# A channel gate streamed in one pass: an 8-row first tile, 26 equal tiles and a TensorE loop

## The chip, the cores and the metric

The kernel runs on one core of a Trainium2 chip. A time is the device time of one execution in microseconds (us), and where several runs are given, it is their median. A profiled execution shows, for every engine and every DMA queue, when each piece of work began and ended. Its span runs from the first to the last instruction of the program and is a little shorter than the time.

## The reference

The input `x` is a bf16 image of 384 x 384 pixels with 384 channels, 113 MB. The output multiplies each channel by a gate that depends on the channel's mean over all pixels:

```python
    g = jnp.einsum("bhwc->bc", x) / (H * W)
    ...
    for i in range(k):
        s = s + gp[:, i:i + C] * w1d[i]
    s = _sigmoid(s)
    return x * s[:, None, None, :]
```

Here `k` is 1, so the gate is `sigmoid(mean * w1d[0])`. All of `x` must be read for the mean before the right gate is known, and all of `x` must be multiplied by it. [...]

## The kernel before

**Layout.** The 147,456 pixels are spread over 128 partitions, which makes 1,152 "rows": one row is one pixel (384 channels, 768 bytes) in each partition. A tile of n rows is a block of n x 128 pixels, and each partition holds n x 768 contiguous bytes of it. The tiles lie in one big buffer, `arena`, in six slots of 44 rows each. Before the change there are 27 tiles: 25 of 44 rows, then one of 28 and one of 24 (`sizes`, line 165).

**An early gate and a check.** The kernel reads and writes the image once. From the first tile alone it forms an early gate, `s_early`, and multiplies every tile with it as it passes. Meanwhile it sums all the other tiles too. At the end it forms the true gate, `s_true`, and compares the two bit for bit, after rounding to bf16. If they differ anywhere, a flag (`redo`) makes SyncE, VectorE and ScalarE run a second pass that loads the whole image again, multiplies it with the true gate and stores it over the first result. The instructions of this second pass (planner `again`, lines 341 to 352) stand behind an `If` in each of the three programs.

**The work of a tile.**
- Load: a DMA from the image to the slot. The first four tiles (`BOTH`, line 115) are loaded in two halves, one issued by SyncE and one by ScalarE; the others are loaded whole by SyncE (`load`, line 169).
- Sum: TensorE multiplies the tile by a matrix of ones in pieces of 512 columns, which adds over the partitions and accumulates in three PSUM banks (`add_rows`, line 199; the matmuls are recorded at line 187). A tile of 44 rows is 33 matmuls. Tile 0 has banks of its own (group 0); all other tiles accumulate in group 1.
- Gate and store: VectorE multiplies the tile by `s_early` (`gate`, line 156, recorded at line 159), in its own slot, and ScalarE issues the DMA that stores it (`put`, line 234). The very last tile is gated into another slot.
- After the sums of a group, VectorE adds the three banks into 384 columns (`add_banks`, line 219), and ScalarE takes the sigmoid (lines 288 and 312). The lines 320 to 334 form the flag.

**What sets the order.** The `Planner` (line 14) holds a list of instructions for each engine. It records for every row of the arena who wrote it last and who has read it since, and puts a wait ahead of an instruction for each of those it depends on (`_needs`, `_wait`). The lists are then written out unrolled: each engine's program is one straight run, with no loop. [...] The loop of line 297 records, for tile k, the gate and store of tile k-6, the load of tile k into the slot that this store sets free, and the sum of tile k. SyncE's queue thus carries loads, and ScalarE's queue carries the halves of the first four tiles, the small weight `w_one`, and then the stores.

Of the kernel before, what the change touches and what calls it, by code (L numbers as in the profile page):

```python
# [13 lines left out]
class Planner:  # L14
# [9 lines left out]
    def __init__(self, nc, name, n_dma_sems):  # L24
        self.nc = nc
        self.streams = {e: [] for e in ("sync", "scalar", "vector", "tensor", "gpsimd")}
        self.sems = {e: nc.alloc_semaphore(f"{name}_{e}") for e in self.COMPUTE}
        self.count = {e: 0 for e in self.COMPUTE}
        self.pool = [nc.alloc_semaphore(f"{name}_dma_{i}") for i in range(n_dma_sems)]
        self.pool_uses = [0] * n_dma_sems  # L30
        self.n_dma = 0
        self.writer = {}
        self.readers = {}
        self.seen = {e: {} for e in self.streams}
        self.final = []

    def _wait(self, engine, token):
        sem, value = token
        if self.seen[engine].get(sem.name, 0) >= value:
            return  # L40
        self.seen[engine][sem.name] = value
        self.streams[engine].append(("wait", sem, value))

    def _needs(self, reads, writes):
        need = {}
        tokens = []
        for r in reads:
            if r in self.writer:
                tokens.append(self.writer[r])
        for r in writes:  # L50
            if r in self.writer:
                tokens.append(self.writer[r])
            tokens.extend(self.readers.get(r, ()))
        for sem, value in tokens:
            if need.get(sem.name, (None, 0))[1] < value:
                need[sem.name] = (sem, value)
        return list(need.values())

    def _record(self, token, reads, writes):
        for r in reads:  # L60
# [5 lines left out]
    def op(self, engine, emit, reads=(), writes=(), signal=True):  # L66


        reads, writes = list(reads), list(writes)
        for token in self._needs(reads, writes):  # L70
            if engine == "tensor" and token[0].name == self.sems["tensor"].name:
                continue
            self._wait(engine, token)
        token = (self.sems[engine], self.count[engine] + 1)
        if signal:
            self.count[engine] += 1
        self.streams[engine].append(("op", emit, self.sems[engine] if signal else None, 1))
        self._record(token, reads, writes)

    def dma(self, engine, out, in_, reads=(), writes=()):  # L80
        reads, writes = list(reads), list(writes)
        for token in self._needs(reads, writes):
            self._wait(engine, token)
        i = self.n_dma % len(self.pool)
        self.n_dma += 1
        if self.pool_uses[i]:
            self._wait(engine, (self.pool[i], 16 * self.pool_uses[i]))
        self.pool_uses[i] += 1
        token = (self.pool[i], 16 * self.pool_uses[i])
        self.streams[engine].append(  # L90
            ("op", lambda e: e.dma_start(out, in_), self.pool[i], 16)  # L91
        )
        self._record(token, reads, writes)
        return token

    def emit(self, name, e, most=None):

        now = self.streams[name][:most]
        del self.streams[name][: len(now)]
        for kind, a, b, *c in now:  # L100
            if kind == "wait":
                e.wait_ge(a, b)
            else:
                ins = a(e)
                if b is not None:
                    ins.then_inc(b, c[0])


def split(n, most):
    k = -(-n // most)  # L110
    return [n // k + (i < n % k) for i in range(k)]


WIDE = 512
EDGE, SLOT, BOTH = 44, 44, 4


def bass_standalone__channel_attn_eca__vision_kernel(
# [12 lines left out]

    ones = nc.alloc_sbuf_tensor("ones", [P, P], BF16)
    s_early = nc.alloc_sbuf_tensor("s_early", [P, C], BF16)
    s_true = nc.alloc_sbuf_tensor("s_true", [P, C], BF16)
    w_one = nc.alloc_sbuf_tensor("w_one", [1, 16], BF16)
    w_scaled = nc.alloc_sbuf_tensor("w_scaled", [P, 2], F32)
    warm = nc.alloc_sbuf_tensor("warm", [P, 2], F32)
    wrong = nc.alloc_sbuf_tensor("wrong", [P, 1], F32)
    redo = nc.alloc_sbuf_tensor("redo", [P, 1], I32)
# [13 lines left out]
    def rows(r0, n):  # L153
        return [("sb", r) for r in range(r0, r0 + n)]
# [3 lines left out]
        v, to_v = (at(r, n).rearrange("p (t c) -> p t c", t=n) for r in (place, to))  # L158
        return lambda e: e.tensor_tensor(to_v, v, s_b, ALU.mult)  # L159

    n_slots = n_arena // SLOT
    full, rest = divmod(n_rows - EDGE, SLOT)
    if rest < EDGE:
        full, rest = full - 1, rest + SLOT
    sizes = [EDGE] + [SLOT] * full + [4 * q for q in split(rest // 4, EDGE // 4)]
    assert sum(sizes) == n_rows and max(sizes) <= SLOT
    plan = Planner(nc, "a", 50)

    def load(place, n, r0, queues=("sync",)):
        of = dram(x_rows, r0, n)  # L170
        i = 0
        for queue, m in zip(queues, split(n, -(-n // len(queues)))):
            plan.dma(
                queue,
                at(place + i, m),
                of[:, i * C : (i + m) * C],
                writes=rows(place + i, m),
            )
            i += m
# [16 lines left out]
            )  # L196
        )

    def add_rows(place, n, group, first, last):

        n_wide = n * C // WIDE
        start = place * C
        for i in range(n_wide):
            bank = acc[group][i % 3]
            plan.op(
                "tensor",
                lambda e, i=i, bank=bank: mm(e,
                    bank[:, :],
                    ones[:],
                    arena[:, start + i * WIDE : start + (i + 1) * WIDE],  # L210
                    start=first and i < 3,
                    stop=last and i >= n_wide - 3,
                ),
                reads=["ones"] + (rows(place, n) if i in (0, n_wide - 1) else []),
                writes=[f"acc{group}"],
                signal=i == n_wide - 1,
            )

    def add_banks(group, copy):

# [10 lines left out]
                )  # L231
            plan.op("vector", emit, reads=[f"acc{group}", "total"], writes=["total"])

    def put(place, n, r0, to):
        plan.op(
            "vector",
            gate(to, place, n, s_early),
            reads=["s_early"] + rows(place, n),
            writes=rows(to, n),
        )  # L240
        plan.final.append(
            plan.dma("scalar", dram(o_rows, r0, n), at(to, n), reads=rows(to, n))
        )

    def weight():
# [12 lines left out]
            reads=["ones", "w_one"],  # L258
            writes=["w_all"],
        )  # L260
        for i, n in enumerate((sizes[0], n_rows)):
            plan.op(
                "vector",
                lambda e, i=i, n=n: e.tensor_scalar_mul(  # L264
# [3 lines left out]
                writes=[f"w_scaled{i}"],  # L268
            )

    starts = [sum(sizes[:k]) for k in range(len(sizes))]
    places = [k % n_slots * SLOT for k in range(len(sizes))]
    last = len(sizes) - 1


    plan.op("gpsimd", lambda e: e.memset(warm[:, 0:1], 0.0), writes=["warm"])  # L276
    plan.op("vector", lambda e: e.memset(ones[:], 1.0), writes=["ones"])  # L277
    for k in range(BOTH):
        load(places[k], sizes[k], starts[k], ("sync", "scalar"))
        if k == 0:  # L280
            plan.dma("scalar", w_one[0:1, 0:1], w1d.unsqueeze(0), writes=["w_one"])
    heads = {e: len(plan.streams[e]) for e in ("sync", "scalar")}
    weight()
    add_rows(places[0], sizes[0], 0, True, True)
    add_banks(0, copy=True)
    plan.op(
        "scalar",
# [3 lines left out]
        reads=["total", "w_scaled0", "warm1"],  # L291
        writes=["s_early"],
    )

    for k in range(1, len(sizes)):
        if k >= n_slots:
            j = k - n_slots
            put(places[j], sizes[j], starts[j], places[j])  # L300
        if k >= BOTH:
            load(places[k], sizes[k], starts[k])
        add_rows(places[k], sizes[k], 1, k == 1, k == last)
    for k in range(len(sizes) - n_slots, last):
        put(places[k], sizes[k], starts[k], places[k])
    put(places[last], sizes[last], starts[last], places[last + 1 - n_slots])


    add_banks(1, copy=False)
    plan.op(  # L310
        "scalar",
        lambda e: e.activation(  # L312
            s_true[:], total[:], ACT_F.Sigmoid, scale=w_scaled[:, 1:2]
        ),
        reads=["total", "w_scaled1"],
        writes=["s_true"],
    )
    plan.op(
        "vector",
        lambda e: e.tensor_tensor(  # L320
            total[:], s_true[:].bitcast(U16), s_early[:].bitcast(U16), ALU.not_equal
        ),
        reads=["s_true", "s_early"],
        writes=["total"],
# [13 lines left out]
    checked = (plan.sems["vector"], plan.count["vector"])  # L338


    again = Planner(nc, "b", 50)
    for place, n, r0 in zip(places, sizes, starts):
        again.dma("sync", at(place, n), dram(x_rows, r0, n), writes=rows(place, n))
        again.op(
            "vector",
# [4 lines left out]
        again.final.append(  # L350
            again.dma("scalar", dram(o_rows, r0, n), at(place, n), reads=rows(place, n))
        )
    for token in again.final:
        again._wait("scalar", token)
    stored = nc.alloc_semaphore("stored")
# [71 lines left out]
```

## Time and profile before

| what | value |
|---|---|
| median of 9 runs | 529.97 us (529.75 to 530.38) |
| time of the profiled execution | 530.1 us |
| its span | 528.6 us |
| mean granted TensorE clock | 0.754 |
| bytes moved by DMA | 226.57 MB, 113.25 MB of them written to HBM |
| mean DMA rate over the span | 429 GB/s |
| first matmul of tile 0 | 14.4 us |
| early gate ready | 27.7 us |
| first store issued | 36.7 us |
| last load issued, and landed | 465.0 and 496.6 us |
| last store issued | 501.6 us |

In the profile's page, a line of a group shows line, engine, operation, destination and source with the shape; then the busy time, the mean duration in ns, the engine's idle time just ahead of these instructions, and what ended most of it. "q1" and "q10" are the queues of SyncE and ScalarE; "q8" and "q14" carry instructions[...]. A line of a window gives the stretch in us, its length, the busy time and number of instructions of PE (TensorE), PEld (its weight loads), DVE (VectorE), ACT (ScalarE) and POOL (GpSimd), then the granted TensorE clock, the mean busy share of the 16 DMA engines, and the GB/s that they moved. SP is SyncE.

### The profile page before, as it was taken

To read this page: it belongs to the slowest core of one execution; us is meant where nothing else is said; L and a number is where in the kernel's file an instruction comes from. 1 tells how busy PE (TensorE), PEld (TensorE's weight loads), DVE (VectorE), ACT (ScalarE), POOL (GpSimd) and SP (SyncE) were. 2 spreads that over 40 slices of the span, in tenths; PEclk is the share of its full clock that TensorE was granted. 3 is DMA by queue.
4 is the path that set the end of the run, shared out by engine and by line. 5 is a ranking of instruction groups with operands and counts; after the bars stand their busy time and mean duration, and the time that the engine had idled before them with its cause. 6 is when DMAs were issued, how large, how long until landed. Compare 5 with 4: busy or idle time off the path is not lost.

```text
span 528.6 us, 1074 instructions
## 1 busy us (share of the span) xinstructions
PE 239.3 (45%) x848; PEld 0.2 (0%) x2; DVE 241.2 (46%) x45; ACT 2.7 (1%) x4; POOL 0.3 (0%) x5
## 2 busy tenths in 40 slices
PE   0976356065164274264264274373263373374400
PEld 0000000000000000000000000000000000000000
DVE  0199742633623624633624614615614615517620
ACT  1000000000000000000000000000000000000000
POOL 0000000000000000000000000000000000000000
PEclk9998786786786875786786876776886876877675
DMA  8999999999999999999999999999999999999998
GB/s 357 431 427 422 442 417 449 422 437 437 422 450 417 442 435 424 442 418 447 432 427 440 419 450 424 435 435 424 447 423 437 435 424 445 418 451 416 442 425 354
DMA packets 8360, 226.57 MB, mean 429 GB/s; under 512 B 930, under 2 KB 930, under 8 KB 930
## 3 DMA queue, kind: packets, MB, share of 16 engines
q10 hardware_dynamic: 4466, 121.90, 53.5%
q1 hardware_dynamic: 3888, 104.60, 46.1%
q8 instruction: 3, 0.05, 0.0%
q14 instruction: 3, 0.02, 0.0%
HBM read 113.25 MB, written 113.25 MB: 428 GB/s over the span
## 4 chain that ended last, share of the span: by engine, by line
another core or an unknown queue 70%; DMA 16%; DVE 4%; PE 3%; issue 1%; SPq 1%; ACT 0%; ACTq 0%
DMA out_dram<-arena 8%; DMA arena<-in_x_dram 6%; PE acc L187 3%; DVE arena L159 2%; DMA w_one<-in_w1d_dram 2%; SPq L91 1%; DVE total L229 1%; ACT s_true L312 0%; ACT s_early L288 0%; DVE total L320 0%; DVE total L227 0%; DVE wrong L328 0%; PE acc L185 0%; ACTq L91 0%
## 5 line engine op out<-in xcount | busy, mean ns | idle before, releaser
L187 PE MATMUL acc<-arena,ones 128*128 128x512 bf16 x846 | 238.8, 448 | 249.2 <-DMA arena<-in_x_dram 246.8
L159 DVE TENSOR_TENSOR arena<-arena,s_early 128x16896 bf16<-128x16896 bf16 (+2 forms) x27 | 234.5, 8692 | 240.0 <-PE acc L187 235.8
L255 PE MATMUL w_all<-w_one,ones 1*128 1x1 bf16 x1 | 0.2, 158 | 14.3 <-DMA w_one<-in_w1d_dram 14.3
L264 DVE TENSOR_SCALAR w_scaled<-w_all 128x1 f32<-128x1 f32 x2 | 0.2, 155 | 13.5 <-PE w_all L255 13.5
L229 DVE TENSOR_TENSOR total<-total,acc 128x128 f32<-128x128 f32 (+2 forms) x11 | 4.5, 408 | 1.6 <-PE acc L187 1.2
L227 DVE COPY total<-acc 128x384 f32<-128x384 f32 x1 | 0.6, 558 | 9.6 <-PE acc L187 9.6
L312 ACT ACTIVATE s_true<-total,w_scaled 128x384 bf16<-128x384 f32 x1 | 0.6, 614 | 477.9 <-DVE total L229 477.9
L249 ACT ACT_TABLE_LOAD x1 | 1.3, 1283 | 3.4 <-issue 3.4
L320 DVE TENSOR_TENSOR total<-s_true,s_early 128x384 f32<-128x384 uint16 x1 | 0.6, 559 | 0.7 <-ACT s_true L312 0.7
L288 ACT ACTIVATE s_early<-total,w_scaled 128x384 bf16<-128x384 f32 x1 | 0.6, 614 | 22.2 <-DVE total L229 22.2
L185 PE MATMUL acc<-arena,ones 128*128 128x512 bf16 x1 | 0.6, 586 | 0.0
L328 DVE TENSOR_REDUCE wrong<-total 128x1 f32<-128x384 f32 x1 | 0.6, 553 | 0.0
L277 DVE MEMSET ones<- 128x128 bf16 x1 | 0.2, 165 | 0.8 <-PEq L412 0.8
L249 ACT ACTIVATE warm<-warm 128x1 f32<-128x1 f32 x1 | 0.2, 202 | 0.0
L334 DVE CAST redo<-wrong 128x1 int32<-128x1 f32 x1 | 0.2, 153 | 0.0
L255 PEld LDWEIGHTS w_all<-w_one,ones 1*128 1x128 bf16 x1 | 0.1, 100 | 14.3 <-issue 14.3
L185 PEld LDWEIGHTS acc<-arena,ones 128*128 128x128 bf16 x1 | 0.1, 105 | 0.0
L412 POOL MEMSET const-bfloat16-1.0<- 128x1 bf16 x1 | 0.1, 102 | 0.0
L412 POOL MEMSET const-uint8-127<- 128x1 uint8 x1 | 0.1, 102 | 0.0
L276 POOL MEMSET warm<- 128x1 f32 x1 | 0.1, 99 | 0.3 <-POOLq L412 0.3
L412 POOL MEMSET const-float32-0.0<- 128x1 f32 x1 | 0.1, 99 | 0.2 <-issue 0.2
L412 POOL MEMSET const-float32-1.0<- 128x1 f32 x1 | 0.1, 99 | 0.0
## 6 DMA issues: line engine op xcount, KB each, us to landing
out_dram<-arena ACTq DMA_DIRECT2D x25, 4224.0 KB, 62.1
arena<-in_x_dram SPq DMA_DIRECT2D x21, 4224.0 KB, 38.7
arena<-in_x_dram ACTq DMA_DIRECT2D x4, 2112.0 KB, 27.4
arena<-in_x_dram SPq DMA_DIRECT2D x4, 2112.0 KB, 26.9
arena<-in_x_dram SPq DMA_DIRECT2D x1, 2688.0 KB, 35.2
out_dram<-arena ACTq DMA_DIRECT2D x1, 2688.0 KB, 30.1
arena<-in_x_dram SPq DMA_DIRECT2D x1, 2304.0 KB
out_dram<-arena ACTq DMA_DIRECT2D x1, 2304.0 KB, 27.0
```

Source lines behind the costliest of these rows:

```text
L91: ("op", lambda e: e.dma_start(out, in_), self.pool[i], 16)
L159: return lambda e: e.tensor_tensor(to_v, v, s_b, ALU.mult)
L185: loaded.append(e.matmul(bank, weights, moving, start=start, stop=stop))
L187: return e.add_instruction(mybir.InstMatmult(name=nc.get_next_instruction_name(), engine=mybir.EngineType.PE, ins=[e.lower_ap(moving), e.l ...
L227: emit = lambda e, part=part, of=of: e.tensor_copy(part, of)
L229: emit = lambda e, part=part, of=of: e.tensor_tensor(part, part, of, ALU.add)
L249: lambda e: e.activation(warm[:, 1:2], warm[:, 0:1], ACT_F.Sigmoid),
L288: lambda e: e.activation(s_early[:], total[:], ACT_F.Sigmoid, scale=w_scaled[:, 0:1]),
L312: lambda e: e.activation(s_true[:], total[:], ACT_F.Sigmoid, scale=w_scaled[:, 1:2]),
L320: lambda e: e.tensor_tensor(total[:], s_true[:].bitcast(U16), s_early[:].bitcast(U16), ALU.not_equal),
L328: lambda e: e.reduce_max(wrong[:], total[:], axis=mybir.AxisListType.X),
L412: nc = _bacc.Bacc("TRN2", target_bir_lowering=False, num_devices=1)
```

## The change

- **Tiles.** The first tile has 8 rows (`FIRST`) and a place of its own behind the six slots (`base`). The other 1,144 rows are 26 tiles of 44. The first tile and the next three (`BOTH = 3`) are loaded in halves on both queues; the loads of tiles 3, 4 and 5 stand behind them on SyncE's queue.
- **The first tile is gated and stored first**, ahead of everything else on VectorE. Every tile, the last one too, is gated in its own slot. `s_true` moves into the first tile's place, once its store is done.
- **Sums.** Tile 0 is summed as before. The 26 others are summed by one loop in TensorE's program: five rounds over the six slots, the last one over two, with an `If` for the other four. Ahead of the loop and after it, three matmuls with zeros open and close the accumulation. In the loop each slot is one wait for a count (`ready`), which is taken down by one, and 33 matmuls, the last of which signals.
- **GpSimd** takes over the waits for the loads: for each tile it waits until the tile has landed and then counts `ready` up by one (`relay`). The planner books the signals of the loop as if it were unrolled (`signals`), so that VectorE waits for the right one.
- **Fewer waits.** The planner now keeps, for each signal, what its engine had seen when it gave it (`clocks`), and drops waits that another wait implies.
- **Second pass.** It goes in 9 tiles of 128 rows through two halves of the slots instead of in 27.

```diff
+    def relay(self, sem, via, to, first, reads, writes):
+
+        if first:
+            self.need(via, first)
+            self.streams[via].append(("op", lambda e: e.sem_inc(sem, 1), None, 0))
+            for name, at in self.seen[via].items():
+                self.seen[to][name] = max(self.seen[to].get(name, 0), at)
+        self.signals(to, reads, writes)
+
+    def signals(self, engine, reads, writes):
+
+        self.count[engine] += 1
+        token = (self.sems[engine], self.count[engine])
+        self._clock(engine, token)
+        self._record(token, reads, writes)
...
-EDGE, SLOT, BOTH = 44, 44, 4
+
+FIRST, TILE, SLOTS, BOTH = 8, 44, 6, 3
...
+    def add_rows(e, group, column, n, at_bank, start, stop):
 
         n_wide = n * C // WIDE
-        start = place * C
         for i in range(n_wide):
...
+            out = mm(
+                e,
+                acc[group][(at_bank + i) % 3][:, :],
+                ones[:],
+                arena[:, column + i * WIDE : column + (i + 1) * WIDE],
+                start and i < 3,
+                stop and i >= n_wide - 3,
             )
+        return out
...
+    def sum_others():
+
+        none = zeros[:, 0:1].broadcast_to([P, WIDE])
+
+        def one(e, s):
+            e.wait_ge(ready, 1).then_inc(ready, -1)
+            add_rows(e, 1, slot(s) * C, TILE, 0, False, False).then_inc(
+                plan.sems["tensor"], 1
+            )
+
+        def emit(e):
+            for i in range(3):
+                mm(e, acc[1][i][:, :], ones[:], none, True, False)
+            rounds = -(-n_tiles // SLOTS)
+            some = n_tiles - (rounds - 1) * SLOTS
+            with e.Fori(0, rounds) as k:
+                for s in range(some):
+                    one(e, s)
+                if some < SLOTS:
+                    with e.If(k < rounds - 1):
+                        for s in range(some, SLOTS):
+                            one(e, s)
+            for i in range(3):
+                out = mm(e, acc[1][i][:, :], ones[:], none, False, True)
+            out.then_inc(plan.sems["tensor"], 1)
+
+        plan.streams["tensor"].append(("block", emit, None))
...
+    load(base, FIRST, 0, ("sync", "scalar"))
+    plan.dma("scalar", w_one[0:1, 0:1], w1d.unsqueeze(0), writes=["w_one"])
     for k in range(BOTH):
-        load(places[k], sizes[k], starts[k], ("sync", "scalar"))
-        if k == 0:
-            plan.dma("scalar", w_one[0:1, 0:1], w1d.unsqueeze(0), writes=["w_one"])
+        load(slot(k), TILE, row0(k), ("sync", "scalar"))
+    for k in range(BOTH, SLOTS):
+        load(slot(k), TILE, row0(k))
...
-    for k in range(1, len(sizes)):
-        if k >= n_slots:
-            j = k - n_slots
-            put(places[j], sizes[j], starts[j], places[j])
-        if k >= BOTH:
-            load(places[k], sizes[k], starts[k])
-        add_rows(places[k], sizes[k], 1, k == 1, k == last)
-    for k in range(len(sizes) - n_slots, last):
-        put(places[k], sizes[k], starts[k], places[k])
-    put(places[last], sizes[last], starts[last], places[last + 1 - n_slots])
+    put(base, FIRST, 0)
+    plan.need("tensor", ["zeros"])
+    sum_others()
+
+    for k in range(n_tiles):
+        if k >= SLOTS:
+            put(slot(k), TILE, row0(k - SLOTS))
+            load(slot(k), TILE, row0(k))
+        there = rows(slot(k), TILE)
+        plan.relay(ready, "gpsimd", "tensor", there, there, ["acc1"])
+    plan.signals("tensor", [], ["acc1"])
+    for k in range(n_tiles - SLOTS, n_tiles):
+        put(slot(k), TILE, row0(k))
...
-    again = Planner(nc, "b", 50)
-    for place, n, r0 in zip(places, sizes, starts):
+    again = Planner(nc, "b", 30)
+    half, r0 = base // 2, 0
+    for k, n in enumerate(split(n_rows, half)):
+        place = k % 2 * half
```

## The prediction

> **What bounds the kernel now.** I read the page's slices and DMA queues first, then the waits, then the chain of waits and short windows at both ends, then the groups of instructions.
>
> ```profile
> span 528.6 us, 1074 instructions
> PE 239.3 (45%) x848; PEld 0.2 (0%) x2; DVE 241.2 (46%) x45; ACT 2.7 (1%) x4; POOL 0.3 (0%) x5
> ...
> DMA  8999999999999999999999999999999999999998
> ...
> q10 hardware_dynamic: 4466, 121.90, 53.5%
> q1 hardware_dynamic: 3888, 104.60, 46.1%
> q8 instruction: 3, 0.05, 0.0%
> q14 instruction: 3, 0.02, 0.0%
> ...
> L187 PE MATMUL acc<-arena,ones 128*128 128x512 bf16 x846 | 238.8, 448 | 249.2 <-DMA arena<-in_x_dram 246.8
> L159 DVE TENSOR_TENSOR arena<-arena,s_early 128x16896 bf16<-128x16896 bf16 (+2 forms) x27 | 234.5, 8692 | 240.0 <-PE acc L187 235.8
> ```
>
> TensorE and VectorE are busy under half of the span; TensorE's idle time is nearly all waiting for loads. The two data queues together take 99.6% of the 16 DMA engines' time. SyncE waits for stores, so a slot's return sets when the next load is issued:
>
> ```profile
> SPq L102 <- DMA out_dram<-arena: 453.4, 21, 62.8
> ```
>
> In the chain of waits that beat is 19.98 us per 44-row tile (86.55, 106.48, 126.48 us and so on). Short windows show the two ends (the last two columns are DMA share and GB/s):
>
> ```profile
> 36.00:496.00 460.00, 214.70 (x759) 0.00 (x0) 221.25 (x26) 0.00 (x0) 0.00 (x0) 0.75 1.00 433
> ...
> 525.50:526.00 0.50, 0.00 (x0) 0.00 (x0) 0.00 (x0) 0.00 (x0) 0.00 (x0) 0.50 0.94 406
> 526.00:526.20 0.20, 0.00 (x0) 0.00 (x0) 0.00 (x0) 0.00 (x0) 0.00 (x0) 0.50 0.23 92
> ...
> 527.00:527.20 0.20, 0.00 (x0) 0.00 (x0) 0.00 (x0) 0.00 (x0) 0.00 (x0) 0.50 0.43 184
> ```
>
> The middle runs at 433 GB/s with a share of 1.00, and the last two microseconds do not: a few DMA engines finish later than the rest. I therefore went through the trace's DMA records one by one. Data packets start at 1.76 us. They take 0.633 us for 16,896 bytes, 0.686 for 18,432, 0.799 for 21,504 and 1.251 for 33,792, which is 36.6 ns per 1,000 bytes plus 0.015. There are 7,424 of them, 464 per DMA engine, and at these prices 524.6 us per engine. To that come 0.7 us for slow first packets and 0.6 around 42 us, where the ACT queue turns from loads to stores; less 1.4 us, because neighbouring packets overlap by some 3 ns. So 1.76 + 524.6 + 1.3 - 1.4 = 526.2 us. Following packets from end to next start, eleven of the engines end between 526.1 and 526.6, and five between 527.2 and 528.1. (The engine a packet ran on is inferred from these times.)
>
> The same records hold six instruction packets inside the span: 16,384 bytes on q8 at 89.8, 229.6 and 389.4 us, and 8,192 bytes on q14 at 492.6 and twice at 513.1. A q8 packet takes 0.96 us, and the next data packet on that engine 1.63 instead of 1.251: 1.33 us per packet. That is the size of the late engines' delay. The last data ends at 528.13, the span at 528.65, and this execution's time was 530.1; the median of nine runs, 529.97, is 0.13 below it. So the end is the same work for all 16 engines, plus what the unluckiest engine carried of instruction loads.
>
> [...] q8's packets have 16,384 bytes and come 140 and 160 us apart, seven to eight tiles of 34 TensorE instructions (33 matmuls and a wait)[...]. [...] at the end 28-row loads ran beside 44-row stores and took 2.75 MB in the 16.3 us from 464.9 to 481.2, 169 GB/s or 39% of 433, which is 21,504/(21,504 + 33,792).
>
> **Part by part.**
>
> Data traffic. Before: 1,024 packets of 16,896 bytes, 256 of 18,432, 256 of 21,504, 5,888 of 33,792. After: 256 of 3,072 (8 rows in two halves), 128 of 6,144 (their store), 768 of 16,896 (tiles 0 to 2 in halves), and (23 + 26) x 128 = 6,272 of 33,792. Again 7,424 packets and the same bytes: 524.6 us per engine, no gain or loss.
>
> Start. No 3,072-byte packet is in the trace. By the line above it costs 0.127 us, an estimate; an engine's first 16 then take 2.0 us. SyncE's second load can issue some 0.4 us after its first, so nothing runs dry. If small packets pay more of the first packet's lag (about 0.7 us) the start loses up to 1 us; a shorter first round could win 0.2. I take +0.2.
>
> Early factor. The 8 rows land near 4.5 us. Six matmuls at up to 0.59 (3.5), the bank sums (24.32 to 27.02, 2.7) and the sigmoid (0.6) put the factor near 11.5 instead of 27.7 us. Worth nothing: the first store stands in the ACT queue behind the halves of tiles 0 to 2. Those end at 1.76 + 0.7 + 2.0 + 3 x 10.1 = 34.8. The 8-row store then alternates with big load packets: 8 x (0.24 + 1.25) = 11.9 us, to 46.7. Tile 0 lands near 14.6, is summed for 9.7 and gated for 9.0, so its store is ready near 34, long before 46.7. The next beats are 20 us each. One load is always queued behind the one in flight.
>
> Tail. Loads 3 to 25 land from 46.7 in beats of 19.98: the last at 486.3 instead of 496.6, with four stores, 40 us, still to go. The last store's turn comes 30 us later. It is now gated in its own slot, so it waits for TensorE: 0.5 us hand-over (estimate) + 9.7 for 33 matmuls (14.5 if all run at the slowest pace, 0.44) + 9.0 gate + 1.1 issue = 20.3 to 25.1. Covered by 5 to 10 us. The bank sums and the comparison (4.7 us, 502.8 to 507.5) and the branch (a fetch 5.6 us later) come by 521 us at the latest.
>
> Waits. GpSimd waits for each tile's loads and counts up; TensorE waits for one count per tile. Nothing else but the remaining counts is queued behind GpSimd's wait. Behind TensorE's waiting instruction stand that tile's 33 matmuls, and VectorE's gate waits for them; in mid-run the gated tile then waits some 40 us for its turn in the store queue (issue to landing 62.1 us, of which its own beat is 20). A late tile costs nothing there. No trace shows such a count[...].
>
> Instruction loads. Unrolled, TensorE has about 900 instructions and three refills. Looped, it has some 20 ahead and a body of 6 x 34 plus control, about 215, run five times with four branches back. [...]
>
> What matters is how many instruction packets the worst engine takes. Three q8 packets before lay on three engines: two on one would have given at least 526.1 + 2.7 = 528.8, later than 528.13. I take more packets, but spread, one on the worst engine: 526.6 + 1.33 + 0.2 = 528.1, + 0.52 to the span's end, + 1.45 outside, - 0.13 to the median = 530.0 us.
>
> **The rivals.**
> - Piled-up refills, slower: [...] Two to three packets on the worst engine: 526.4 + 2.7 to 4.0 + 1.84 = 530.9 to 532.2; four to five: 533.5 to 534.9. It decides as soon as one engine carries two more 16 KB packets than the others. [...] Against: successive fetches did change engines. I price it at 532.
> - No refills in the run, faster: [...] The worst engine ends at 526.6: 526.6 + 1.84 = 528.4, with the start's 0.2 528.6. [...] Against: three fetches before.
> - A slow start from small packets, or a late last tile, beyond the covers above: 531 to 532. The second pass, were it run, would add over 500 us; the weight of these inputs is 0.0012, so the early factor's error is about 1.5e-6 at 0.5, far below a bf16 step there. Negligible.
>
> **How the numbers follow.** What can be told from no change is about 0.2%, 1.06 us. Forecast (spread refills) 0.45, of which 0.37 within 0.2%, 0.03 faster and 0.05 slower; piled up 0.30, slower; no refills 0.20, of which 0.16 faster by over 0.2% and 0.04 within; slow start or tail 0.05, slower. Sum: faster 0.19, same 0.41, slower 0.40. The forecast's own range is 529.2 to 531.0. The full one reaches from 528.4 (no refills) to 533.2, leaving out the top of the pile-up.
>
> **What would show it.** Data queues still near 99.6% together; 7,424 data packets; loads ending near 486 us; middle still 433 GB/s. The step at stake is the q8 line: one packet or none says "no refills", 5 to 13 says the branches refetch, and the windows after 526 us say whether one engine trails. An empty DMA stretch in the middle, or a last store waiting for its gate, would make the whole argument wrong.

## The result and the profile after

The changed kernel takes 537.15 us (median of 10 runs, 532.06 to 541.99) beside 529.92 us for the kernel before: a ratio of 1.0129, 95% interval 1.011 to 1.0148. It is slower, and it scatters over 10 us where the kernel before scatters over 0.7. The prediction of 530.0 us with a range up to 533.2 was wrong. The ratios in this document leave out runs more than 1.5% above the fastest of the same kernel, so where the scatter is the effect itself they understate it, and the range says more.

The page of the changed kernel, in the lines that answer to those shown of before:

```profile
span 535.3 us, 1096 instructions
PE 237.6 (44%) x854; PEld 0.2 (0%) x2; DVE 241.1 (45%) x45; ACT 2.7 (1%) x4; POOL 0.3 (0%) x6
...
DMA  8999999999999999999999999999999999999995
...
q10 hardware_dynamic: 4466, 120.13, 52.1%
q1 hardware_dynamic: 3888, 106.37, 46.7%
q8 instruction: 1, 0.02, 0.0%
q14 instruction: 2, 0.02, 0.0%
...
L237 PE MATMUL acc<-arena,ones 128*128 128x512 bf16 x846 | 235.5, 443 | 262.1 <-PEq L276 259.8
```

The compute engines do the same work in the same time. The instruction queue q8, on which the prediction staked its doubt, carries one packet instead of three, at 499.1 us, and none near the loop's four branches back. What changed is the last digit of the DMA line, 5 instead of 8. Windows show it, first the middle, then the end (the last two columns are DMA share and GB/s):

```profile
100.00:200.00 100.00, 44.65 (x162) 0.00 (x0) 42.60 (x6) 0.00 (x0) 0.00 (x0) 0.74 1.00 429
200.00:300.00 100.00, 43.45 (x158) 0.00 (x0) 43.25 (x5) 0.00 (x0) 0.00 (x0) 0.74 1.00 430
...
526.00:528.00 2.00, 0.00 (x0) 0.00 (x0) 0.00 (x0) 0.00 (x0) 0.00 (x0) 0.50 0.74 321
528.00:530.00 2.00, 0.00 (x0) 0.00 (x0) 0.00 (x0) 0.00 (x0) 0.00 (x0) 0.50 0.28 118
530.00:532.00 2.00, 0.00 (x0) 0.00 (x0) 0.00 (x0) 0.00 (x0) 0.00 (x0) 0.50 0.12 51
532.00:534.00 2.00, 0.00 (x0) 0.00 (x0) 0.00 (x0) 0.00 (x0) 0.00 (x0) 0.50 0.16 68
```

The same stretches of the kernel before:

```profile
100.00:200.00 100.00, 45.96 (x161) 0.00 (x0) 43.08 (x6) 0.00 (x0) 0.00 (x0) 0.74 1.00 433
200.00:300.00 100.00, 45.56 (x162) 0.00 (x0) 45.35 (x6) 0.00 (x0) 0.00 (x0) 0.74 1.00 432
...
526.00:528.00 2.00, 0.00 (x0) 0.00 (x0) 0.00 (x0) 0.00 (x0) 0.00 (x0) 0.50 0.22 92
528.00:530.00 2.00, 0.00 (x0) 0.00 (x0) 0.00 (x0) 0.00 (x0) 0.00 (x0) 0.50 0.00 0
```

Twelve of the 16 DMA engines end at 527.2 to 528.9 us, about 1 us later than before (526.1 to 528.1 for all 16), two more by 532.0, and the last two, a share of some 0.12 to 0.16, go on until 534.6 and 534.9. The middle gives 429 to 430 GB/s at a share of 1.00, against 432 to 433 before: the engines are not idle there, some of their packets take longer.

The DMA records say which. Below, packets of 33,792 bytes are followed from end to next start, so that each line is one DMA engine from 84 to 130 us (L a load's packet, S a store's; "excess" is what its packets took beyond 1.251 us each):

```
changed kernel                                              excess, us
84.32 SLSLLSLSLSLSLSLSSLSLLSLSLSLSLSLSSLSLL                 0.00   (6 engines alike, 0.00 to 0.04)
84.71 LSLSLLSLSLSLSLSSLSLSLLSLSLSLSLSSLSLSL                 0.00   (7 engines alike, 0.00 to 0.02)
85.12 SLSLLSLSLSLSLSLSSLSLLSLSLSLSLSLSSLSL                  0.45
84.28 LSSLLSLSLSLSLSLSLSSLLSLSLSLSLSLSLSSL                  1.17
84.30 LSSLLSLSLSLSLSLSLSSLLSLSLSLSLSLSLSSL                  1.16
kernel before
84.42 SLSLSLSLSLSLSLSLSLSLSLSLSLSLSLSLSLSLS                 0.00   (13 of 16 engines in this pattern)
```

"SS" marks the end of a load on that engine (a record of 4 bytes, 0.009 us, one for each transfer and engine, takes a turn there), "LL" the end of a store. In the kernel before nearly all engines end both together. In the changed kernel loads end two to three packets ahead of stores, and not on all engines alike. Two engines, 0.03 us apart, are a packet behind, and in every tile some of their packets are stretched by 0.15 to 0.4 us, on both engines at the same moments (near 91.9, 107.2, 112.4 and 127.7 us). The time between the first and the last engine's completion of one load grows from 3.0 us at 66 us to 9.9 at 373, and is 9.8 at 494. Before, it is 2.5 us at first, 3.6 after the instruction packet at 90 us, and 3.8 at the end. The packets of 33,792 bytes that took more than 0.04 us beyond 1.251 us add up to 3.4 us per engine, against 0.6 before.

The start shows where the two queues part. The timeline of the kernel before, and that of the changed kernel:

```profile
0.73 0.41 ACTq L91 DMA_DIRECT2D arena<-in_x_dram  x1
...
1.17 0.55 ACTq L91 DMA_DIRECT2D w_one<-in_w1d_dram  x1
1.74 1.58 ACTq L91 DMA_DIRECT2D arena<-in_x_dram  x3
```

```profile
0.73 0.41 ACTq L109 DMA_DIRECT2D arena<-in_x_dram  x1
0.73 0.10 POOL L351 MEMSET warm<- 128x1 f32 x1 [0.29 <-POOLq L493]
0.73 3.89 SPq L109 DMA_DIRECT2D arena<-in_x_dram  x7
...
1.17 0.54 ACTq L109 DMA_DIRECT2D w_one<-in_w1d_dram  x1
1.74 1.90 ACTq L109 DMA_DIRECT2D arena<-in_x_dram  x3
```

ScalarE issues the 2-byte load of the weight between its first two halves, as it did before. Before, its first half was 22 rows, 10 us of work for the queue. Now it is 4 rows, done on 13 of 16 engines by 4.2 us and on the last at 5.04, and the next half's first packet starts only at 5.99, SyncE's at 3.90. For a time SyncE's queue alone is served: from 6 us on it is 2.9 packets per engine ahead, and at 480 us still 3.0, though hardly a packet is stretched after 400 us (0.07 of the 3.4 us per engine). In the kernel before this lead is 0.2. I call it the lead below (packets begun on q1 less those on q10, per engine, from the DMA records).

### The profile page after: what moved, and what is told of

Same layout as the page of the kernel before. It is cut to its first block, busy times and chain, and to the rows that moved or that the text cites. A ratio compares the mean times of both kernels' runs of the same rounds, so it can differ in the third digit from the quotient of the medians.

```text
span 535.3 us, 1096 instructions
## 1 busy us (share of the span) xinstructions
PE 237.6 (44%) x854; PEld 0.2 (0%) x2; DVE 241.1 (45%) x45; ACT 2.7 (1%) x4; POOL 0.3 (0%) x6
## 5 line engine op out<-in xcount | busy, mean ns | idle before, releaser
L201 DVE TENSOR_TENSOR arena<-arena,s_early 128x16896 bf16<-128x16896 bf16 (+1 forms) x27 | 234.5, 8691 | 267.9 <-PE acc L237 267.3
L237 PE MATMUL acc<-arena,ones 128*128 128x512 bf16 x846 | 235.5, 443 | 262.1 <-PEq L276 259.8
L237 PE MATMUL acc<-zeros,ones 128*128 128x512 bf16 x6 | 1.9, 441 | 0.0
L235 PE MATMUL acc<-arena,ones 128*128 128x512 bf16 x1 | 0.6, 586 | 0.5 <-DMA arena<-in_x_dram 0.5
```

The source lines that it names most:

```text
L235: loaded.append(e.matmul(bank, weights, moving, start=start, stop=stop))
L237: return e.add_instruction(mybir.InstMatmult(name=nc.get_next_instruction_name(), engine=mybir.EngineType.PE, ins=[e.lower_ap(moving), e.l ...
```

## The experiments

Each of these kernels ran beside the kernel before, of which the first row gives all 194 runs. The lead leaves out the 768-byte packets that some kernels add. "Spread" is first to last engine's completion of a load, early (near 66 us) and at the last tile. Lead and spread come from one profiled run of each kernel, which need not be a typical one: it took 541.22 us for unrolled, 572.06 for after_less1, 541.47 for after_dram, 531.56 for after_layout and 529.84 for after_more2.

| kernel | median, us (range) | ratio (95%) | lead at 100 us | spread, us |
|---|---|---|---|---|
| before | 529.93 (529.56 to 530.50) | 1 | 0.2 | 2.5, 3.8 |
| after | 537.15 (532.06 to 541.99) | 1.0129 (1.011 to 1.0148) | 2.8 | 3.0, 9.8 |
| unrolled | 532.71 (531.72 to 541.22) | 1.0044 (1.0027 to 1.006) | 2.6 | 3.2, 15.4 |
| before_loop | 529.89 (529.68 to 530.0) | 0.9998 (0.9989 to 1.0007) | 0.1 | 2.3, 3.4 |
| weight_later | 529.78 (529.27 to 530.72) | 0.9998 (0.9989 to 1.0007) | 1.0 | 3.0, 3.0 |
| weight_gpsimd | 529.79 (529.44 to 530.78) | 1.0 (0.9991 to 1.0009) | 0.8 | 1.4, 1.4 |
| after_evened | 529.83 (529.58 to 530.46) | 1.0 (0.9991 to 1.0009) | -1.4 | 3.4, 3.7 |
| after_less1 | 551.94 (530.08 to 572.17) | 1.0036 (1.0016 to 1.0057) | 0.3 | 1.9, 23.5 |
| after_more2 | 530.37 (529.84 to 538.25) | 1.0033 (1.0006 to 1.0059) | 4.9 | 3.2, 3.1 |
| before_extra1 | 530.16 (530.0 to 530.22) | 1.0004 (0.9995 to 1.0013) | 2.2 | 2.9, 3.4 |
| before_extra2 | 530.08 (530.06 to 530.34) | 1.0004 (0.9995 to 1.0013) | 2.3 | 2.4, 2.9 |
| before_extra3 | 530.15 (529.97 to 530.44) | 1.0006 (0.9997 to 1.0015) | 4.0 | 2.5, 3.1 |
| before_extra5 | 530.2 (529.99 to 533.64) | 1.0011 (1.0 to 1.0023) | 4.1 | 2.0, 1.8 |
| before_three | 530.19 (529.88 to 534.91) | 1.001 (1.0 to 1.002) | 5.9 | 0.6, 1.7 |
| before_gap | 530.27 (529.89 to 531.07) | 1.0008 (1.0001 to 1.0015) | 5.9 | 1.9, 1.8 |
| after_rotated | 539.11 (537.82 to 540.43) | 1.0166 (1.0141 to 1.019) | 2.6 | 3.3, 14.2 |
| after_layout | 534.07 (531.56 to 539.19) | 1.0111 (1.0048 to 1.0175) | 2.9 | 2.9, 5.4 |
| after_dram | 539.0 (531.41 to 541.47) | 1.0124 (1.0039 to 1.021) | 2.5 | 3.1, 7.2 |
| after_bare | 538.79 (538.69 to 540.87) | 1.0168 (1.0151 to 1.0185) | 1.7 | 1.9, 7.9 |
| before_bare | 528.65 (528.47 to 529.24) | 0.9977 (0.9969 to 0.9985) | 0.1 | 2.8, 2.8 |

**Is it the loop?** Two kernels separate the loop from the tiles. In unrolled the changed kernel's loop and counts are replaced by

```diff
-    plan.need("tensor", ["zeros"])
-    sum_others()
...
-        plan.relay(ready, "gpsimd", "tensor", there, there, ["acc1"])
+        plan.op(
+            "tensor",
+            lambda e, k=k: add_rows(
+                e, 1, slot(k) * C, TILE, 0, k == 0, k == last
+            ),
+            reads=["ones"] + there,
+            writes=["acc1"],
+        )
```

> The changed kernel with TensorE's sums unrolled again, each tile waiting for its loads itself; no loop, no counts from GpSimd. Loop theory (the loop or GpSimd's counting disturbs the DMA engines): back to 529 to 530 us. Lead theory (SyncE's load queue runs 2.8 packets per DMA engine ahead of ScalarE's queue, against 0.2 before, and loads and stores that are out of step slow each other): still 534 to 540 us, landings of a tile's load spread over some 10 us at the end.

and before_loop puts such a loop on the old tiles:

```diff
+            with e.Fori(0, n_loop // n_slots):
+                for s in range(n_slots):
+                    e.wait_ge(ready, 1).then_inc(ready, -1)
...
-        add_rows(places[k], sizes[k], 1, k == 1, k == last)
+        if k <= n_loop:
+            there = rows(places[k], sizes[k])
+            plan.relay(ready, "gpsimd", "tensor", there, there, ["acc1"])
+        else:
+            add_rows(places[k], sizes[k], 1, False, k == last)
```

> The kernel before with its tiles, and the sums of its 24 full tiles after the first as a loop of four rounds over the six slots, let on by counts from GpSimd. Loop theory: 534 to 540 us. Lead theory: lead stays 0.2, no slow-down, 528.5 to 530.2 us, and fewer instruction packets on q8 than the three of before.

The unrolled kernel is slow (531.7 to 541.2 us), the loop on the old tiles isn't (529.89). The page of before_loop has one q8 packet, as the changed kernel has, and the end of unrolled trails as that of the changed kernel does:

```profile
q8 instruction: 1, 0.02, 0.0%
```

```profile
528.00:530.00 2.00, 0.00 (x0) 0.00 (x0) 0.00 (x0) 0.00 (x0) 0.00 (x0) 0.50 0.51 220
530.00:532.00 2.00, 0.00 (x0) 0.00 (x0) 0.00 (x0) 0.00 (x0) 0.00 (x0) 0.50 0.27 118
532.00:536.00 4.00, 0.00 (x0) 0.00 (x0) 0.00 (x0) 0.00 (x0) 0.00 (x0) 0.50 0.16 68
```

So neither the loop, nor GpSimd's counts, nor the smaller number of instruction packets is needed for the slow-down. Four of unrolled's five runs took 531.7 to 532.8 us, less than the changed kernel's median, so this run alone leaves open whether they add to it; after_bare (below), which has none of them, is at 538.79.

**Is it the start of the two queues?** weight_later moves one line:

```diff
     load(base, FIRST, 0, ("sync", "scalar"))
-    plan.dma("scalar", w_one[0:1, 0:1], w1d.unsqueeze(0), writes=["w_one"])
     for k in range(BOTH):
         load(slot(k), TILE, row0(k), ("sync", "scalar"))
+        if k == 0:
+            plan.dma("scalar", w_one[0:1, 0:1], w1d.unsqueeze(0), writes=["w_one"])
```

> The changed kernel with the small load of the weight issued after ScalarE's half of tile 0 instead of ahead of it, so that the half is issued 0.6 us earlier and ScalarE's queue has less of a gap; loop and tiles stay. Lead theory: the lead falls from 2.8 packets towards 0 to 1, and the time to 528.3 to 531 us. Loop theory and small-tile theory: unchanged, 534 to 540 us.

529.78 us, and the lead is 1.0. The timeline and the windows of weight_later:

```profile
0.73 0.89 ACTq L109 DMA_DIRECT2D arena<-in_x_dram  x2
...
0.73 3.84 SPq L109 DMA_DIRECT2D arena<-in_x_dram  x7
```

```profile
100.00:200.00 100.00, 45.60 (x162) 0.00 (x0) 45.38 (x6) 0.00 (x0) 0.00 (x0) 0.74 1.00 433
200.00:300.00 100.00, 47.07 (x162) 0.00 (x0) 45.38 (x6) 0.00 (x0) 0.00 (x0) 0.71 1.00 433
...
526.00:528.00 2.00, 0.00 (x0) 0.00 (x0) 0.00 (x0) 0.00 (x0) 0.00 (x0) 0.50 0.04 17
```

ScalarE's half of the first 44-row tile (tile 0 in these expectations) is issued 0.6 us earlier, its first packet starts at 4.68 us instead of 5.99, and 7 us at the other end of the run are gone: the middle is back at 433 GB/s and no engine trails. The weight itself arrives later and delays nothing: the early gate is ready at 22.3 us instead of 11.7. weight_gpsimd takes the weight to a third queue (`plan.dma("gpsimd", w_one[0:1, 0:1], ...)`):

> The changed kernel with the weight loaded from GpSimd's own queue, so that ScalarE can issue its half of tile 0 at 1.2 us, as SyncE does. Start theory: the lead falls below 1 packet and the time to 528.5 to 530 us. If the lead stays or the small load disturbs the engines: 531 to 540 us.

529.79 us, with the smallest spread of all at the last tile, 1.4 us; it ties with the kernel before. Other kernels with the changed start took 531.4 us or more in every run beside them: unrolled beside weight_later, after_layout and after_dram beside weight_gpsimd.

**Is it the lead as such?** The kernel before with three halves instead of four (`BOTH = 3`) gets a lead of 4 to 6 packets from ScalarE's queue running dry at 34 us:

> The kernel before with three tiles loaded in halves instead of four; nothing else. ScalarE's queue then runs dry near 34 us and the first store comes near 37.5, so SyncE's queue should get 2 to 3 packets per engine ahead, with the old tiles and no loop. Lead theory: slower, 533 to 540 us, stretched loads in mid-run. Loop theory and small-tile theory: no change, 529.5 to 530.5 us.

530.19 us: hardly slower. Here the lead theory, as I had put it, failed. Next I set the lead without any gap, by small loads in one queue, one packet of 768 bytes per 16 partitions and engine. On the old tiles (1, 2, 3 and 5 packets):

```diff
+    plan.dma("scalar", at(264, 1)[0 : 16 * 3, :], x_rows[0 : 16 * 3, :], writes=rows(264, 1))
     heads = {e: len(plan.streams[e]) for e in ("sync", "scalar")}
```

> The kernel before with one more small load on ScalarE's queue behind its four halves: 32 partitions of 768 bytes into an unused row, two small packets for each DMA engine. Nothing stops and no queue has a gap, but from there on SyncE's loads should be 2 packets per engine ahead of ScalarE's stores. Offset theory (loads that run 2 to 3 packets of 8 ahead of the stores slow each other, as in the changed kernel): 531 to 540 us. Gap theory (the engines were driven apart by ScalarE's queue running dry at the start, and never came together again): 529.7 to 530.3 us.

> The same with three small packets for each engine (48 partitions). Offset theory: 531 to 540 us, lead 3 packets in the trace, stretched loads in mid-run. Gap theory: 529.7 to 530.3 us.

> The same with five small packets for each engine (80 partitions). The kernel before with three halves had a lead of 4 to 6 packets and 530.2 us; so both theories: 529.7 to 530.6 us. A time above 531 would say that the lead matters, but not only between 2 and 3.

> The kernel before with one small packet per DMA engine more on ScalarE's queue (16 partitions of 768 bytes into an unused row). The additions of 2, 3 and 5 came out at leads of about 2 to 4, 4 and 4 to 6 packets and none was slow, so a lead that stays between 2 and 3 has not been tried on the old tiles. Narrow offset theory (only a lead that stays between 2 and 3 packets slows): lead near 2, 531 to 540 us. Theory that the new tiles or the start of the changed kernel are needed as well: 529.8 to 530.3 us.

All have medians of 530.1 to 530.2 us. before_extra1 comes near the lead and the spread of the changed kernel (2.2 packets and 2.9 us, against 2.8 and 3.0), with nearly the same pattern on every engine, and doesn't drift: 3.3 us at 122 us, 3.4 at 494. On the old tiles such leads cost 0.3 us or less in the median. They are not quite free of the effect, though: one run of 12 of before_extra5 took 533.64 us and one of 20 of before_three 534.91, where none of the 194 runs of the kernel before is above 530.50. On the new tiles, with the gap at the start left in place:

```diff
+    plan.dma("sync", at(base + FIRST, 1)[0 : 16 * 3, :], x_rows[0 : 16 * 3, :], writes=rows(base + FIRST, 1))
     for k in range(BOTH, SLOTS):
```

> The changed kernel, its gap at the start untouched, with three small packets for each engine added to SyncE's queue behind its half of tile 2 (48 partitions of 768 bytes into an unused row), so that loads and stores come back into step. Offset theory: lead near 0, 529 to 530.2 us. Gap theory: still 532 to 540 us.

> The changed kernel with one small packet per engine added to SyncE's queue ahead of its full tiles, so that its lead falls by about one packet, to 1 to 2. Narrow offset theory: 529.5 to 531 us. If any remaining lead of this kind slows in proportion: 532 to 535 us.

> The changed kernel with two small packets per engine added to ScalarE's queue behind its halves, so that the lead grows from 2.8 to 4 or 5. Narrow offset theory: 529.5 to 531 us, since the kernel before was hardly slowed at such leads. Theory that in the changed kernel every lead is bad and only the return into step helped: 534 to 542 us.

Three packets for SyncE's queue cure it (529.83), though the changed kernel itself didn't run beside it. One packet makes it much worse: runs from 530 to 572 us, 6 of 21 below 532. In the profiled one two engines, 0.02 us apart, have every store packet stretched by 0.11 to 0.64 us between 76 and 107 us, both at the same moments, while their load packets keep 1.251 us. The last load's spread is 23.5 us, and the lead falls from 0.3 packets at 100 us to -7.8 at 400. Two packets for ScalarE's queue cure most runs (7 of 12 below 530.5), the others are at 531.3 to 538.3. So the lead that the start leaves changes how bad it gets, in no simple order, and a lead near zero is no protection by itself.

**Is it where the data lie?** Three edits change addresses only: the outputs moved on by a tile, the arena back at its old SBUF address, the tiles back at their old rows of the image.

```diff
-            put(slot(k), TILE, row0(k - SLOTS))
+            put(slot(k), TILE, row0((k - SLOTS + 1) % n_tiles))
...
-        put(slot(k), TILE, row0(k))
+        put(slot(k), TILE, row0((k + 1) % n_tiles))
```

> The changed kernel with every 44-row tile stored one tile further on in the output (the last one to the first tile's place): the output is another one than the reference's, and the amount of work and its order are the same. It changes by one tile the distance in memory between what is loaded and what is stored at a time. If the slow-down comes from where loads and stores fall in HBM relative to each other, and a tile's length matters for it: 529.5 to 531 us. If it comes from the order of packets in the queues alone, or only from the place within a tile: still 534 to 542 us.

```diff
+    s_true = nc.alloc_sbuf_tensor("s_true", [P, C], BF16)[:]
     w_one = nc.alloc_sbuf_tensor("w_one", [1, 16], BF16)
...
-    zeros = nc.alloc_sbuf_tensor("zeros", [P, 2], BF16)
...
+    zeros = nc.alloc_sbuf_tensor("zeros", [P, 2], BF16)
...
-    s_true = at(base, 1)
```

> The changed kernel with the true gate in a tensor of its own and the zeros behind the arena, so that the arena starts at the same SBUF address as in the kernel before. Start theory (the two queues start unevenly, engine by engine, and two engines that fall a packet behind then slow each other for the whole run): still 532 to 542 us. If the tiles' SBUF addresses matter: 529.3 to 530.5 us.

```diff
-        return FIRST + k * TILE
+        return k * TILE
...
-    load(base, FIRST, 0, ("sync", "scalar"))
+    load(base, FIRST, n_rows - FIRST, ("sync", "scalar"))
...
-    put(base, FIRST, 0)
+    put(base, FIRST, n_rows - FIRST)
```

> The changed kernel with its 8-row tile taken from the end of the image, so that the 44-row tiles start at multiples of 44 rows, as in the kernel before; the early gate comes from other rows. Start theory: still 532 to 542 us. If the tiles' place in HBM matters: 529.3 to 530.5 us.

All three stay slow (medians 539.11, 534.07 and 539.0 us). In after_dram it isn't a pair: from 88 to 92 us all 16 engines have packets stretched by 0.2 to 0.8 us.

**Does a gap at the start do it on the old tiles?** ScalarE waits for its first half to land before it issues the second:

```diff
             plan.dma("scalar", w_one[0:1, 0:1], w1d.unsqueeze(0), writes=["w_one"])
+            plan._wait("scalar", plan.writer["sb", places[0] + sizes[0] - 1])
```

> The kernel before, in which ScalarE waits for its half of tile 0 to land before it issues its half of tile 1; its queue then runs dry for some 2 us at 13 us and the engines get different numbers of SyncE's packets ahead, 2 to 4. Start theory: 531 to 540 us, with two engines that lag together. If the new tiles' addresses are needed: 529.8 to 530.4 us.

530.27 us. ScalarE's queue was empty from 12.9 to 17.0 us, longer than expected, and the gap gave every engine the same lead of 6 packets; all 16 show one pattern, and none drifts. This spoke against the start theory as written: a gap alone is not enough.

**Is anything but the image's traffic needed?** after_bare and before_bare keep loads, early gate, gates and stores. From the edit of after_bare:

```diff
-    plan.need("tensor", ["zeros"])
-    sum_others()
...
-        plan.relay(ready, "gpsimd", "tensor", there, there, ["acc1"])
...
-    add_banks(1, copy=False)
...
-            second_pass("sync", e)
```

> The changed kernel without the sums of its 26 tiles, without GpSimd's counts, the true gate, the comparison and the second pass; loads, early gate, gates and stores stay. Start theory (only the way the two queues of loads and stores start matters): still slow, 530.5 to 542 us, with two or more engines that drift behind. If TensorE's reads, the loop or the signals are needed for it: 528.4 to 529.8 us.

> The kernel before without the sums of tiles 1 to 26, without the true gate and its comparison and without the second pass; loads, early gate, gates and stores stay. By the prediction's sum, an end without instruction packets is 1.3 to 1.5 us earlier: 528.4 to 528.8 us, no q8 packet. If instruction packets cost nothing at the end: 529.8 to 530.1 us.

The pages of after_bare and of before_bare:

```profile
span 539.2 us, 156 instructions
PE 2.9 (1%) x7; PEld 0.2 (0%) x2; DVE 237.6 (44%) x36; ACT 2.1 (0%) x3; POOL 0.3 (0%) x6
...
q10 hardware_dynamic: 4466, 120.13, 51.8%
q1 hardware_dynamic: 3888, 106.37, 47.2%
```

```profile
span 527.1 us, 212 instructions
...
q10 hardware_dynamic: 4466, 121.90, 53.6%
q1 hardware_dynamic: 3888, 104.60, 46.2%
```

Neither has a line for q8 or q14. Without any work of TensorE on the 26 tiles the changed kernel is still at 538.79 us, with packets stretched on all 16 engines (0.4 to 1.2 us per engine between 84 and 130 us). Loads, stores and the gates between them are enough for the slow-down. The kernel before gets 1.29 us faster (528.65 beside 529.94) when it is stripped so. That its instruction packets cost this much fits the ends of its DMA engines, which now all lie at 525.9 to 526.7 us, while before five of 16 ended at 527.2 to 528.1; it is not shown alone, as the sums went too.

## Why the prediction was wrong

**The step that failed is "Start".** It said that SyncE's second load can issue some 0.4 us after its first, "so nothing runs dry", and took 0.2 us. I looked at SyncE's queue only. ScalarE's has the weight's load between its halves, and the change cut the work that used to hide it from 10 us to 3: q10 stood empty on all engines from 5.0 to 6.0 us, and on most since 4.2. The empty stretch itself cost little, as SyncE's packets filled the engines: by the DMA records they were idle for 0.10 us each between 2 and 6 us, against 0.02 before. What I had no term for is that the engines leave it out of step, two to three packets and not all alike, and that packets are then stretched for hundreds of us, in the profiled run until some 400. I had priced a late start at 1 us at most; moving that one issue is worth 7.4 us (537.15 to 529.78). That the start is the trigger is shown by weight_later and weight_gpsimd, which move only the weight's load. The length of the gap doesn't give the size of the loss: in after_bare q10 was empty on all engines for only 0.25 us.

**Data traffic** was right in packets (7,424 before and after) and wrong in their price: "no gain or loss" held for the median packet (1.251 us), and the stretching of packets of 33,792 bytes added 2.8 us on the mean engine (3.4 less 0.6) and more on the worst, whose last packet ended at 534.9 us instead of 528.1. The small packets were priced well: 0.121 us for 3,072 bytes (estimated 0.127), 0.234 for 6,144 (0.240).

**Early factor**: ready at 11.7 us, forecast 11.5, and worth nothing, as weight_later shows, which has it at 22.3.

**Tail**: covered, with less to spare than forecast. The last sum ended near 504.5, the gate at 513.5, and the last store was issued at 513.9; the first engine was done with the store before it at 517.2. That is 3.3 us of cover instead of 5 to 10, as the loads ended at 494 instead of 486.

**Waits**: a tile landed at 107.3 us and its sum began at 107.76, so the count through GpSimd took 0.5 us, as estimated, and hid.

**Instruction loads**: wrong in number, about right in price. I expected 5 to 13 q8 packets and got one. That a branch back would fetch was my estimate: the kernel before has no loop, so its trace could not show it, and in the changed kernel no packet is seen near the four branches back. The one at 499.1 us took 0.93 us, and the next data packet on that engine 1.64 instead of 1.251: 1.32 us together, where I had 1.33. The price of 1.3 to 1.5 us for the worst engine's packets fits the 1.29 of before_bare. Going from three packets to one gains none of it: before_loop with one is at 529.89, the kernel before with three at 529.93. That it is the one on the last engine that counts is argued, not tested alone.

**The rivals**: the slower one, piled-up refills, had the sign and not the mechanism. "A slow start from small packets" had the place but a price of 1 to 2 us and a chance of 0.05.

**Open** is which resource the engines contend for, if it is that, why three packets on SyncE's queue cure the run and one worsens it, and what the old tiles have that keeps them together at the same lead in all but two runs. Ruled out as sole causes are the output's tile, the arena's address, the image's rows, TensorE's work on the 26 tiles and the instruction packets. That the stretched packets of two engines slow each other is suggested by their falling at the same moments, and not shown. That an uneven lead from engine to engine matters is suggested by before_gap and before_extra1, where it is even; after_evened, uneven and fast, speaks against it as the whole answer.

## What to carry to other kernels

When two queues feed the same DMA engines in a stream that is bound by them, check at a change of the first transfers that neither queue runs dry, and count every issue between them: here a transfer that was hidden under 10 us of queued work lay open under 3. The middle of such a run can lose most of a per cent (429 to 430 against 432 to 433 GB/s) with all engines at a share of 1.00, so look at the GB/s of long windows, at the last microseconds engine by engine, and at the scatter of the runs. Cutting a program's instruction packets from three to one gained nothing that could be told here (529.89 against 529.93 us).

## What the runs showed of the hardware

- One program, unchanged, ran from 530 to 572 us (after_less1). In its run of 572.06 us every store packet on two DMA engines took 0.11 to 0.64 us beyond 1.251 us between 76 and 107 us, on both at the same moments, and no load packet on them did.
- A lead of one queue over the other lasted on the old tiles: with one to five small packets or a gap at 13 us, it was at 400 us within 0.4 packets of what it was at 100 us. In after_less1, whose engines drifted apart, it moved by eight (0.3 to -7.8).
- A loop of some 200 TensorE instructions, run four or five times, had one packet on q8, near its end (469.5 us in before_loop, 499.1 in the changed kernel), and none at the branches back before.
- A half tile issued by ScalarE at 1.74 us had its first packet at 5.99, with SyncE's seven loads issued beside it, and one issued at 1.2 had it at 4.7 (weight_later, weight_gpsimd). So early in these runs the way from issue to first packet was 3.5 to 4.3 us; for the very first load, issued at 0.73, it was 1.0.
